# Half of x of batch 0 loaded by hardware queues and cast on chip, x of batch 1 in halves, a new order up to slice 40, and sums of e made on GpSimd

## The chip, the core and the metric

The kernel runs on one core of a Trainium2 chip. A core has TensorE (PE, with its weight load PEld), VectorE (DVE), ScalarE (ACT), GpSimd (POOL) and SyncE (SP), which work through queues of their own, and 16 DMA engines. DMAs issued by SP and ACT go through hardware queues, those issued by GpSimd through a software queue, which can cast float32 to bfloat16 on the way. The metric is the device time of the whole kernel in microseconds, lower is better.

## The reference

Eight batches of cross attention between 512 tokens `x` and 32 state rows per head (8 heads of 64), in both directions, followed by one gated layer over all rows:

```python
scores = scale * x @ state.T;   a  = softmax(scores);   xread = a @ state
scores2 = scale * state @ x.T;  a2 = softmax(scores2);  sread = a2 @ x
rows = concatenate([xread, sread], axis=2)        # (B, H, 512 + 32, 64) -> (4352, 512)
gate = maximum(rows @ w_gate, 0);  val = rows @ w_val   # 512 -> 1536
out = (gate * val) @ w_out                              # 1536 -> 512
```

## The kernel before

Work is in bfloat16 with float32 sums in PSUM. For a batch b, `att_sc` makes the scores for a half kc of the heads, `att_exp` their exponentials `e_sn` (ACT), `att_sum` and `att_scale` the softmax over the states, `a_sn` (DVE). `a_sn` is turned to `ANS`, by PE (`att_T`, `att_out`) in the first three batches and by a DMA transpose later. The value product is folded into the weights: U = state @ w_gate and state @ w_val per head (`c_unit` and `u_unit` on PE, `c_out` and `u_out` to SBUF), so that `gv(b, jf)` gives slice jf (of 12, 128 columns each) of both hidden halves in two PSUM banks. `relu` (ACT) and `mult` (DVE) turn them into `h_sb`. The output product is done in 14 half products a batch (`o_half`, a Winograd scheme of seven products), for which GpSimd makes sums of hidden blocks (`h_sums`, `h_last`, tiles `s`) and of weight blocks (`w_sum`, tiles `t1`, `t2w`, `t4`). PSUM has a ring of six banks for all but the two output accumulators.

The other direction is `sr_mm(b)`: PE multiplies x with `e_sn`, and with `sel`, a matrix of ones for one half of the partitions, it adds `e_sn` over all 512 tokens: for each parity, half kc and group c of 128 tokens one matmul, 16 a batch. `sr_norm` divides one by the other into `br`. These rows go through the hidden layer at the end (`gvs`, `s_step`).

The order is written by hand. A prologue issues the DMAs: the state of the first two batches on SP; on GpSimd's queue x of batch 0 in two halves with a cast, pieces of 256 columns of w_gate and w_val in turn, x of batches 1 and 2 with a cast, the other states, w_out and x of batch 3. A ring of eight semaphores makes a GpSimd DMA wait for the eighth before it. A string `program` then gives the order up to slice 40 (batch 3, slice 4): words such as `xT.0.3` (transpose x of batch 0, head pair 3), `xo.0.3.dve` (its copy, on DVE), `sc.0.0`, `c.0.4`, `co` (copy of U), `ga` and `gb` (the two halves of gv), `re`, `mu`, `oh.0.2`, `hs`, `hl`, `ws`, `nx` (att_scale), `srm` and `srn` (sr_mm, sr_norm), and `spin.n`, n matmuls on an empty tile `warm`. After that a loop over slices runs each output half product 18 slices behind its gv, and `at(b, jf, ...)` hangs the attention of the next batch and the rest on given slices.

Of the kernel before, what the change touches and what calls it, by code (L numbers as in the profile page):

```python
# [16 lines left out]
def kernel(  # L17
# [182 lines left out]
    def att_scale(b, kc):  # L200
        e_v = e_sn[b][:, kc].rearrange("p c (h n) -> p (c h) n", n=Ns)
        nc.vector.tensor_tensor(out=a_sn[b][:, kc].rearrange("p c (h n) -> p (c h) n", n=Ns), in0=e_v,  # L202
                                in1=held["rc", b, kc].to_broadcast([128, NC * HK, Ns]), op=ALU.mult)
# [20 lines left out]
    def sr_mm(b):  # L224

        ps = held["sr", b] = bank("sr_ps")
        e = e_sn[b].rearrange("p k c (j s n) -> p k c j s n", j=2, s=2)
        for kc in range(NK):
            for c in range(NC):
                for j2 in range(2):  # L230
                    j = 2 * kc + j2
                    if b in cast_on_load:
                        for h2 in range(2):
                            q = slot(j, h2)
                            nc.tensor.matmul(ps[64 * h2:64 * h2 + 64, 64 * j + 32 * q:64 * j + 32 * q + 32],
                                             xb[b][:, c, 2 * j + h2], e[:, kc, c, j2, q],
                                             start=(kc == 0 and c == 0 and j2 == 0), stop=False, skip_group_check=True)
# [4 lines left out]
        for parity in range(2):
            for kc in range(NK):
                for c in range(NC):
                    nc.tensor.matmul(ps[:, 256 + 64 * kc:320 + 64 * kc], sel[:, parity],  # L245
                                     e[:, kc, c, :, slot(2 * kc, parity)],
                                     start=False, stop=(parity == 1 and kc == 1 and c == NC - 1), skip_group_check=True)
# [238 lines left out]
    nc.vector.memset(warm, 0.0)
# [42 lines left out]
    program = """
    spin.7 stc.0.2.dve stT.0.2 sto.0.2.1.dve xT.0.0 xT.0.1 xo.0.1.dve xT.0.3 xo.0.3.dve sto.0.2.0.dve  # L530
    xo.0.0.act sc.0.0 ex.0.0 xT.0.2 spin.1 xo.0.2.dve sc.0.1 spin.1 ex.0.1 nr.0.0 c.0.0 nx.0.0 aT.0.0 nr.0.1
    nx.0.1 co.0.0.1.act c.1.0 ao.0.0.act aT.0.1 co.0.0.0.act ga.0.0 co.1.0.1.dve c.0.1 co.1.0.0.act c.1.1
    ao.0.1.dve gb.0.0 co.0.1.0.act ga.0.2 co.1.1.0.act co.0.1.1.dve gb.0.2 re.0.0 mu.0.0 ga.0.3 gb.0.3
    co.1.1.1.dve ga.0.1 gb.0.1 re.0.2 mu.0.2 xT.1.0 re.0.3 mu.0.3 xT.1.2 re.0.1 mu.0.1 xT.1.1 xo.1.1.dve
    xT.1.3 xo.1.3.dve c.0.2 co.0.2.1.dve xo.1.0.act sc.1.0 c.1.2 co.1.2.0.dve xo.1.2.act co.0.2.0.act sc.1.1
    ga.0.4 ga.0.5 gb.0.5 ex.1.0 co.1.2.1.act ex.1.1 c.0.3 gb.0.4 nr.1.0 nx.1.0 aT.1.0 re.0.5 co.0.3.0.act
    mu.0.5 ao.1.0.dve re.0.4 nr.1.1 c.1.3 co.1.3.1.act c.0.4 ga.0.6 co.0.4.0.dve nx.1.1 co.0.3.1.act gb.0.6
    co.1.3.0.act mu.0.4 ga.0.7 co.0.4.1.act re.0.6 gb.0.7 re.0.7 aT.1.1 ao.1.1.dve mu.0.7 ga.0.9 mu.0.6 gb.0.9
    ga.0.8 gb.0.8 re.0.9 ga.1.0 gb.1.0 ga.1.1 gb.1.1 ga.1.6 mu.0.9 re.0.8 re.1.0 mu.1.0 re.1.1 mu.1.1 gb.1.6
    re.1.6 ga.1.3 gb.1.3 mu.0.8 re.1.3 ga.1.2 stT.2.4 mu.1.6 gb.1.2 re.1.2 ga.1.5 gb.1.5 sto.2.4.0.act mu.1.3  # L540
    re.1.5 ga.1.4 mu.1.5 gb.1.4 ga.1.7 gb.1.7 oh.0.0 sto.2.4.1.act re.1.7 re.1.4 xT.2.0 xT.2.2 mu.1.2 c.0.5
    co.0.5.0.act xT.2.3 mu.1.7 xT.2.1 mu.1.4 xo.2.2.dve co.0.5.1.dve xo.2.1.dve c.1.5 hs.0.0 hs.0.1 ga.0.11
    co.1.5.0.dve co.1.5.1.dve xo.2.0.act gb.0.11 re.0.11 mu.0.11 xo.2.3.act ga.0.10 gb.0.10 oh.0.1 sc.2.0
    ga.1.10 gb.1.10 re.0.10 mu.0.10 ws.0.pool ex.2.0 ga.1.11 gb.1.11 re.1.10 re.1.11 u.2.1.0 uo.2.1.0.1.act
    nr.2.0 mu.1.10 uo.2.1.0.0.act nx.2.0 mu.1.11 c.1.4 sc.2.1 ex.2.1 oh.0.2 oc.0.1 u.2.0.0 aT.2.0 ws.1.pool
    co.1.4.0.dve hs.0.2 nr.2.1 ga.1.8 xc.3.0.pool xc.3.1.pool co.1.4.1.act nx.2.1 oh.0.4 uo.2.0.0.0.act gb.1.8
    ws.2.pool re.1.8 oh.0.3 oh.0.5 mu.1.8 xd.4 ga.1.9 oa.0.3 ao.2.0.dve ws.3.pool gb.1.9 hl.0 hs.1.0
    xc.4.0.pool xc.4.1.pool aT.2.1 oh.0.6 ao.2.1.act ga.2.0 uo.2.0.0.1.dve xt.3 re.1.9 mu.1.9 gb.2.0 ga.2.1
    hs.1.2 xt.4 re.2.0 mu.2.0 gb.2.1 re.2.1 ga.2.3 gb.2.3 hs.1.1 ga.2.2 re.2.3 mu.2.3 oc.0.5 gb.2.2 re.2.2
    oh.0.7 oh.0.8 u.2.1.1024 mu.2.1 uo.2.1.1024.0.dve u.2.0.1024 uo.2.0.1024.0.dve oh.0.9 u.2.1.512  # L550
    uo.2.1.512.0.dve uo.2.0.1024.1.act u.2.0.512 oc.0.9 oa.0.9 oh.0.10 oh.0.11 uo.2.0.512.0.act ga.2.5 oh.0.12
    oc.0.11 mu.2.2 ga.2.4 uo.2.0.512.1.dve oh.1.0 uo.2.1.512.1.act gb.2.4 gb.2.5 oh.0.13 xd.5 re.2.4 mu.2.4
    re.2.5 sc.3.0 oh.1.1 srm.0 os.0.11 ga.2.7 ex.3.0 ga.2.6 oa.0.13 mu.2.5 uo.2.1.1024.1.act gb.2.6 nr.3.0
    srn.0 re.2.6 mu.2.6 sc.3.1 ex.3.1 gb.2.7 re.2.7 mu.2.7 nr.3.1 nx.3.0 nx.3.1 aD.3 oc.1.1 ga.2.8 gb.2.8
    u.3.0.0 hs.2.0 oh.1.2 re.2.8 mu.2.8 u.3.0.512 uo.3.0.0.0.act uo.3.0.512.0.act uo.3.0.0.1.dve u.3.1.0
    oh.1.3 hl.1 oa.1.3 oh.1.4 uo.3.1.0.1.dve uo.3.1.0.0.act ga.2.9 uo.3.0.512.1.dve gb.2.9 srm.1 re.2.9 oh.1.5
    mu.2.9 oc.1.5 ga.2.10 srn.1 gb.2.10 re.2.10 mu.2.10 xc.5.0.pool ga.2.11 stT.4.8 sto.4.8.1.act
    sto.4.8.0.dve gb.2.11 re.2.11 mu.2.11 oh.1.6 oh.1.7 u.3.1.1024 uo.3.1.1024.0.act u.3.1.512
    uo.3.1.512.1.dve u.3.0.1024 uo.3.1.512.0.act oh.1.8 uo.3.0.1024.1.dve ga.3.0 gb.3.0 uo.3.0.1024.0.act
    hs.2.1 hs.2.2 ga.3.1 xc.5.1.pool re.3.0 gb.3.1 re.3.1 ga.3.3 oh.1.9 mu.3.0 mu.3.1 oc.1.9 oa.1.9  # L560
    uo.3.1.1024.1.dve ga.3.2 gb.3.2 re.3.2 srm.2 gb.3.3 re.3.3 oh.1.10 mu.3.2 oh.1.11 sc.4.0 ex.4.0 srn.2
    nr.4.0 nx.4.0 oc.1.11 os.1.11 xt.5 mu.3.3 xd.6
    """
# [91 lines left out]
```

## Time and profile before

| | |
|---|---|
| median of the runs | 227.91 us (227.42 to 228.1, 3 runs) |
| profiled execution | 226.67 us, span 224.9 us |
| PE busy | 212.3 us |
| GpSimd busy | 149.9 us |
| first gv matmul | 13.76 us |
| first product with w_out | 35.93 us |
| last PE matmul of the chain ends | 220.60 us |

The span is what the trace covers; the profiled execution's own time is 1.8 us longer. Starts are microseconds from the span's start. A row in order of time gives start, duration, engine, line, operation and tiles, and in brackets the idle time before it and what ended it. Line numbers are those of the kernel before; in the changed kernel the same lines stand further down.

### The profile page before, as it was taken

The numbers are of one execution on the slowest core, as the hardware profiler recorded it, in microseconds if no ns is written. First come the engines' busy times: TensorE is split into PE (matmuls) and PEld (weight loads), VectorE is DVE, ScalarE is ACT, GpSimd is POOL, SyncE is SP. The second block draws the span as 40 slices with busy tenths as digits, with TensorE's granted clock in tenths as the row PEclk, the third lists the DMA queues.
The fourth block names the chain that finished last, engine by engine and source line by source line (L and its number), as shares of the span: only waits on it lengthen the run. The fifth ranks groups of instructions, "written<-read, shape, count | busy, mean of one in ns | idle before, by whom it ended". The sixth has DMA issues, their size and how long they took to land.

```text
span 224.9 us, 5527 instructions
## 1 busy us (share of the span) xinstructions
PE 212.3 (94%) x2219; PEld 140.1 (62%) x2251; DVE 160.0 (71%) x278; ACT 120.1 (53%) x226; POOL 149.9 (67%) x141
## 2 busy tenths in 40 slices
...
GB/s 94 171 192 196 197 195 271 62 50 278 3 111 266 138 3 85 201 230 4 62 227 228 3 72 184 74 3 91 63 82 1 81 62 47 4 95 50 47 26 208
DMA packets 42329, 25.06 MB, mean 111 GB/s; under 512 B 18784, under 2 KB 41824, under 8 KB 42304
## 3 DMA queue, kind: packets, MB, share of 16 engines
...
## 4 chain that ended last, share of the span: by engine, by line
PE 78%; DMA 8%; DVE 5%; issue 3%; ACT 2%; POOL 2%; another core or an unknown queue 0%; ACTq 0%; DVEq 0%; POOLq 0%
PE gv_ps L299 30%; PE w_ps L394 18%; PE z_ps L394 13%; DMA wv_sb<-in_moe_w_val_dram 5%; PE gv_ps L317 5%; PE up L274 4%; DMA wg_sb<-in_moe_w_gate_dram 3%; PE sr_ps L245 2%; ACT g_sb L326 2%; PE zs_ps L394 1%; DVE h_sb L330 1%; DVE a_sn L202 1%; PE ws_ps L394 1%; PE sc_ps L186 1%; PE sr_ps L240 1%
## 5 line engine op out<-in xcount | busy, mean ns | idle before, releaser
L330 DVE TENSOR_TENSOR h_sb<-gv_ps,g_sb 128x512 bf16<-128x512 f32 (+1 forms) x108 | 69.0, 656 | 35.1 <-ACT g_sb L326 26.1
L299 PE MATMUL gv_ps<-ans,U 128*128 128x512 bf16 x353 | 92.1, 379 | 1.9 <-DVE U L294 0.2
L326 ACT ACTIVATE g_sb<-gv_ps 128x512 bf16<-128x512 f32 (+1 forms) x108 | 61.9, 576 | 44.2 <-PE gv_ps L299 21.1
L394 PEld LDWEIGHTS <-h_sb 128*128 128x128 bf16 x510 | 49.4, 98 | 15.9 <-issue 1.5
L360 POOL TENSOR_TENSOR s<-h_sb 128x512 bf16<-128x512 bf16 x24 | 28.1, 1172 | 43.9 <-DVE h_sb L330 43.8
L299 PEld LDWEIGHTS <-U 128*128 128x128 bf16 x384 | 35.7, 98 | 31.1 <-issue 0.8
L369 POOL TENSOR_TENSOR h_sb<-h_sb,s 128x512 bf16<-128x512 bf16 x24 | 27.0, 1154 | 7.3 <-PE z_ps L394 7.3
L404 ACT COPY o_sb<-w_ps 128x512 f32<-128x512 f32 x32 | 18.8, 586 | 21.9 <-PE w_ps L394 19.2
L361 POOL TENSOR_TENSOR s<-s,h_sb 128x512 bf16<-128x512 bf16 x24 | 28.0, 1167 | 1.9
L362 POOL TENSOR_TENSOR h_sb<-h_sb 128x512 bf16<-128x512 bf16 x24 | 28.1, 1172 | 0.0
L394 PE MATMUL w_ps<-wo_sb,h_sb 128*128 128x256 bf16 x192 | 26.2, 273 | 0.0
L284 ACT CAST U<-up 128x512 bf16<-128x512 f32 x37 | 19.9, 595 | 11.8 <-PE up L274 11.8
L394 PE MATMUL z_ps<-wo_sb,h_sb 128*128 128x256 bf16 x186 | 24.4, 273 | 0.0
L394 PEld LDWEIGHTS <-s 128*128 128x128 bf16 x204 | 19.2, 98 | 7.7 <-issue 2.8
L284 DVE CAST U<-up 128x512 bf16<-128x512 f32 x35 | 22.3, 682 | 1.6 <-PE up L274 1.5
L410 DVE TENSOR_TENSOR o_sb<-z_ps,o_sb 128x512 f32<-128x512 f32 (+1 forms) x23 | 15.5, 673 | 4.5 <-PE z_ps L394 2.7
L196 DVE TENSOR_REDUCE cs<-e_sn 128x16 f32<-128x512 bf16 x16 | 10.8, 678 | 5.6 <-ACT e_sn L190 5.6
L202 DVE TENSOR_TENSOR a_sn<-e_sn,rc 128x512 bf16<-128x512 bf16 x16 | 14.2, 893 | 0.4
L190 ACT ACTIVATE e_sn<-sc_ps 128x512 bf16<-128x512 f32 x16 | 9.6, 600 | 8.5 <-PE sc_ps L186 8.4
L394 PE MATMUL w_ps<-t2w,s 128*128 128x256 bf16 x96 | 13.1, 273 | 0.1
L394 PE MATMUL z_ps<-t,s 128*128 128x256 bf16 x90 | 12.0, 273 | 0.1
L394 PE MATMUL w_ps<-t,h_sb 128*128 128x256 bf16 x96 | 12.0, 273 | 0.0
...
## 6 DMA issues: line engine op xcount, KB each, us to landing
...
xf<-in_x_dram SPq DMA_DIRECT2D x4, 1024.0 KB, 6.8
...
xb<-in_x_dram POOLq DMA_DIRECT2D x2, 512.0 KB, 10.6
xf<-in_x_dram POOLq DMA_DIRECT2D x1, 1024.0 KB, 19.5
...
```

What stands on the lines that cost most here:

```text
L202: nc.vector.tensor_tensor(out=a_sn[b][:, kc].rearrange("p c (h n) -> p (c h) n", n=Ns), in0=e_v, in1=held["rc", b, kc].to_broadcast([128, ...
L284: copy[eng](out=U[b][:, w, kc, lo:lo + 512], in_=held["u", b, w, lo][kc])
L299: nc.tensor.matmul(ps[w], U[b][:, w, kc, f0:f0 + 128], ANS[b][:, kc].rearrange("p c t -> p (c t)"), start=(kc == 0), stop=(kc == NK - 1))
L326: nc.scalar.activation(out=g_sb[:, 0:n], in_=ps[0][:, 0:n], func=AF.Relu)
L330: nc.vector.tensor_tensor(out=dst, in0=ps[1][:, 0:n], in1=held["g", b, jf][:, 0:n], op=ALU.mult)
L360: tt(out=s_block(b, 1, i), in0=a21, in1=a22, op=ALU.add)
L361: tt(out=s_block(b, 2, i), in0=s_block(b, 1, i), in1=a11, op=ALU.subtract)
L362: tt(out=a21, in0=a11, in1=a21, op=ALU.subtract)
L369: {"dve": nc.vector, "pool": nc.gpsimd}[eng].tensor_tensor(out=a12, in0=a12, in1=s_block(b, 2, i), op=ALU.subtract)
L394: nc.tensor.matmul(ps[:, HM * c:HM * c + HM], a[:, i, 128 * c:128 * c + 128], w[:, i], start=(i == 0 and (p in ("p1", "p2", "p5") and c == ...
L404: nc.scalar.copy(out=o_sb, in_=held["acc", b, "w", 0])
L410: nc.vector.tensor_tensor(out=o_sb[:, cols], in0=banks[c if isinstance(c, int) else 0][:, cols], in1=o_sb[:, cols], op=ALU.add)
```

## The change

x of batch 0: heads 0 and 1 come as float32 on ACT's hardware queue, heads 2 and 3 on SP's behind the state, heads 4 to 7 on GpSimd's queue with a cast as before. Two new steps `xh.0.dve` and `xh.1.act` cast the first four heads. x of batch 1 comes in two DMAs. x of batch 3 is issued by a step `xg.3`. `sr_pre` adds the four token groups of `e_sn` on GpSimd in float32 (three passes over 128x256) and has ACT round the sum to bfloat16; `sr_low` has GpSimd write what the rounding left. `sr_mm` then uses these two parts, 8 matmuls with `sel` instead of 16, for the batches that have them: 3 to 7. `att_scale` can run on GpSimd, and does for (2, 1), (3, 1) and (4, 0); the casts (3, 0) and (5, 0) of x go from GpSimd to ACT. The program is in a new order, with three more warm-up matmuls.

```diff
+    def sr_pre(b):
+        t = small.tile([128, NK, 128], FP32, name="es_f", tag="es_f", bufs=1)
+        for c in range(1, NC):
+            nc.gpsimd.tensor_tensor(out=t, in0=t if c > 1 else e_sn[b][:, :, 0], in1=e_sn[b][:, :, c], op=ALU.add)
+        es = held["es", b] = small.tile([128, 2, NK, 128], BF16, name="es", tag="es", bufs=1)
+        nc.scalar.copy(out=es[:, 0], in_=t)
+        held["es_f", b] = t
+
+    def sr_low(b, eng="pool"):
+        es = held["es", b]
+        {"dve": nc.vector, "pool": nc.gpsimd}[eng].tensor_tensor(out=es[:, 1], in0=held["es_f", b], in1=es[:, 0],
+                                                                op=ALU.subtract)
...
+        if ("es", b) in held:
+            for parity in range(2):
+                for kc in range(NK):
+                    for part in range(2):
+                        es = held["es", b][:, part, kc].rearrange("p (j s n) -> p j s n", j=2, s=2)
+                        nc.tensor.matmul(ps[:, 256 + 64 * kc:320 + 64 * kc], sel[:, parity],
+                                         es[:, :, slot(2 * kc, parity)],
...
+    x0_dma(nc.scalar, xf[0], 0, 2)
     state_dma(nc.sync, st_f, 0, 2)
-    x_dma_cast(0, 2)
+    x0_dma(nc.sync, xf[0], 2, 4)
+    x0_dma(nc.gpsimd, xb0, 4, H)
...
         if i == 1:
-            x_dma_cast(1)
+            x_dma_cast(1, 2)
...
-    x_dma(3, (nc.gpsimd,))
...
-    spin.7 stc.0.2.dve stT.0.2 sto.0.2.1.dve xT.0.0 xT.0.1 xo.0.1.dve xT.0.3 xo.0.3.dve sto.0.2.0.dve
+    stc.0.2.dve spin.7 stT.0.2 sto.0.2.1.act spin.1 xh.0.dve spin.1 xT.0.0 sto.0.2.0.dve xh.1.act xT.0.1
...
     for b in range(3, B):
+        at(*((b, 5) if b < B - 1 else (b, 2)), sr_pre, b)
+        at(*((b, 5) if b < B - 1 else (b, 2)), sr_low, b, "pool")
         at(*((b + 1, 0) if b < B - 1 else (b, 4)), sr, b)
```

GpSimd's queue at the start (`xb` is x in bfloat16, `id` and `sel` are constants, `wg_sb` and `wv_sb` the weights), before:

```order
L116 DMA xb<-in_x_dram 128x4x256 x2
masks.py:197 MEMSET id_94 128x128
...
L120 DMA wv_sb<-in_moe_w_val_dram 128x4x256
L116 DMA xb<-in_x_dram 128x8x256
L120 DMA wg_sb<-in_moe_w_gate_dram 128x4x256
```

and with the change:

```order
L520 DMA xb<-in_x_dram 128x4x256
masks.py:197 MEMSET id_94 128x128
...
L120 DMA wv_sb<-in_moe_w_val_dram 128x4x256
L116 DMA xb<-in_x_dram 128x4x256 x2
L120 DMA wg_sb<-in_moe_w_gate_dram 128x4x256
```

One x DMA fewer stands ahead of the constants and weights, and one more between the second and the third pair of weights.

DVE's queue at the start (`stT` is the turned state, `xT` the turned x), before:

```order
L487 MEMSET stT 128x1024
L129 CAST st_b<-st_f 128x256
L143 COPY stT<-stT_ps 64x2x2x32 x2
L175 COPY xT<-xT_ps 128x4x128 x2
L143 COPY stT<-stT_ps 64x2x2x32 x2
L175 COPY xT<-xT_ps 128x4x128
```

and with the change:

```order
L512 MEMSET stT 128x1024
L129 CAST st_b<-st_f 128x256
L523 CAST xb<-xf 128x512
L143 COPY stT<-stT_ps 64x2x2x32 x2
L175 COPY xT<-xT_ps 128x4x128 x3
L196 TENSOR_REDUCE cs<-e_sn 128x16
```

A cast of x comes in, and the state's second pair of copies has gone to ACT, so that none stands behind copies of x.

GpSimd in the middle of the program, from the third `h_sums` of batch 0 to the first of batch 1, before:

```order
L362 TENSOR_TENSOR h_sb<-h_sb 128x2x256
L151 CAST xb<-xf 128x4x4x64 x2
L338 TENSOR_TENSOR t_100<-wo_sb,t2w 128x1536
L338 TENSOR_TENSOR wo_sb<-wo_sb 128x6x256
L369 TENSOR_TENSOR h_sb<-h_sb,s_775 128x2x256 x3
L360 TENSOR_TENSOR s_970<-h_sb 128x512
```

and with the change, where the casts of batch 4 also move ahead of batch 1's sums:

```order
L387 TENSOR_TENSOR h_sb<-h_sb 128x2x256
L151 CAST xb<-xf 128x4x4x64
L202 TENSOR_TENSOR a_sn<-e_sn,rc 128x512
L363 TENSOR_TENSOR t_100<-wo_sb,t2w 128x1536
L363 TENSOR_TENSOR wo_sb<-wo_sb 128x6x256
L394 TENSOR_TENSOR h_sb<-h_sb,s_686 128x2x256 x3
L151 CAST xb<-xf 128x4x4x64 x2
L385 TENSOR_TENSOR s_997<-h_sb 128x512
```

One cast of x has become a multiplication `a_sn`; the other cast of batch 3 is on ACT.

More of the change, by code (lines that the diff above doesn't have):

```diff
@@ L198, in att_sum, with att_scale @@
         nc.vector.reciprocal(out=rc, in_=cs)
-    def att_scale(b, kc):
+    def att_scale(b, kc, eng="dve"):
         e_v = e_sn[b][:, kc].rearrange("p c (h n) -> p (c h) n", n=Ns)
-        nc.vector.tensor_tensor(out=a_sn[b][:, kc].rearrange("p c (h n) -> p (c h) n", n=Ns), in0=e_v,
+        (nc.gpsimd if eng == "pool" else nc.vector).tensor_tensor(out=a_sn[b][:, kc].rearrange("p c (h n) -> p (c h) n", n=Ns), in0=e_v,
                                 in1=held["rc", b, kc].to_broadcast([128, NC * HK, Ns]), op=ALU.mult)
@@ L241, in sr_mm @@
                                      start=(kc == 0 and c == 0 and j2 == 0), stop=False, skip_group_check=True)
+        if ("es", b) in held:
[5 more added lines that the diff above has]
+                                         es[:, :, slot(2 * kc, parity)],
+                                         start=False, stop=(parity == 1 and kc == 1 and part == 1),
+                                         skip_group_check=True)
+            return
         for parity in range(2):
@@ L487, with x0_dma, x0_cast @@
     nc.vector.memset(stT, 0.0)
+    cast_on_load.add(0)
+    xb_alloc(0)
+    xf[0] = xin.tile([128, H, NC, D], FP32, name="xf", tag="xf")
+    xb0 = xb[0].rearrange("p (h c d) -> p h c d", h=H, c=NC)
+    xb[0] = xb[0].rearrange("p (h c d) -> p c h d", h=H, c=NC)
+    def x0_dma(eng, dst, lo, hi):
+        eng.dma_start(out=dst[:, lo:hi], in_=x[0, lo:hi].rearrange("h (p c) d -> p h c d", c=NC))
+    def x0_cast(i, eng):
+        copy[eng](out=xb0[:, 2 * i:2 * i + 2], in_=xf[0][:, 2 * i:2 * i + 2])
+    x0_dma(nc.scalar, xf[0], 0, 2)
     state_dma(nc.sync, st_f, 0, 2)
-    x_dma_cast(0, 2)
+    x0_dma(nc.sync, xf[0], 2, 4)
+    x0_dma(nc.gpsimd, xb0, 4, H)
     nc.scalar.activation(out=tiny, in_=nc.const_aps.tensor(0.0, (128, 1), FP32), func=AF.Exp)
@@ L526 @@
              "gb": lambda b, jf: gv(b, jf, (1,)), "re": relu, "mu": mult, "oh": o_half, "oc": o_c, "oa": o_a, "os": o_s,
-             "hs": h_sums, "hl": h_last, "ws": w_sum, "xd": lambda b: x_dma(b, (nc.sync,)), "xc": x_cast,
-             "xt": x_trans_dma, "aD": att_aT_dma, "srm": sr_mm, "srn": sr_norm}
+             "hs": h_sums, "hl": h_last, "ws": w_sum, "xd": lambda b: x_dma(b, (nc.sync,)), "xg": lambda b: x_dma(b, (nc.gpsimd,)),
+             "xh": x0_cast, "xc": x_cast,
+             "xt": x_trans_dma, "aD": att_aT_dma, "srp": sr_pre, "srl": sr_low, "srm": sr_mm, "srn": sr_norm}
@@ L535 @@
[L535 to L559, printed above, removed]
```

41 lines of the change are left out of this document (33 added, 8 removed).

## The prediction

> **What bounds the kernel now.** I read the page's busy times, then the stages, then the chain of waits, then the first 15 us and the GpSimd lane in order of time. The sum below is made against the profiled execution: 226.67 us, of which 224.9 are span. The runs' median is 227.91, 1.24 above it, so I take differences from the profile and apply them to the median. A difference under 0.3% (0.7 us) can't be told from none.
>
> ```profile
> PE 212.3 (94%) x2219; PEld 140.1 (62%) x2251; DVE 160.0 (71%) x278; ACT 120.1 (53%) x226; POOL 149.9 (67%) x141
> ```
> ```profile
> 2.00:3.00 1.00, 1.00 (x4) 0.43 (x3) 0.21 (x2) 0.22 (x2) 1.00 (x3) 1.00 0.66 118
> 3.00:4.00 1.00, 1.00 (x4) 0.18 (x2) 0.34 (x1) 0.00 (x0) 0.87 (x5) 1.00 0.97 97
> 4.00:5.00 1.00, 0.93 (x5) 0.40 (x4) 0.04 (x1) 0.00 (x0) 1.00 (x4) 1.00 1.40 186
> ...
> 64.00:75.00 11.00, 9.89 (x168) 6.56 (x170) 10.47 (x17) 5.24 (x11) 10.77 (x10) 1.00 1.06 227
> ...
> 100.00:120.00 20.00, 19.84 (x211) 13.27 (x213) 16.32 (x28) 11.10 (x21) 13.25 (x13) 1.00 0.45 116
> ```
> The columns are the stretch, its length, the busy time of PE, PEld, DVE, ACT and POOL, granted clock, DMA share and GB/s. In the steady loop PE is busy 19.84 of 20 us: work taken off PE there is time. In 64 to 75 PE lacks 1.1 us, and GpSimd is full. The start is another regime, by the chain of waits:
>
> ```profile
> 5.54 6.76 DMA wg_sb<-in_moe_w_gate_dram
> ...
> 12.58 11.98 DMA wv_sb<-in_moe_w_val_dram
> ```
> From 5.54 to 24.56 the chain is weights on their way.
>
> **Term 1, the start.** These rows are in order of time (start, duration, engine, line, operation, and in brackets the wait before it).
>
> ```profile
> 0.74 0.45 SPq L95 DMA_DIRECT2D st_f<-in_state_dram  x1
> 1.19 3.17 PE L516 MATMUL warm_ps<-warm 128*128 128x512 bf16 x7 [1.19 <-DVE warm L486]
> 1.27 1.70 POOL L116 DMA_DIRECT2D xb<-in_x_dram  x2 [0.82 <-POOLq L639]
> 3.00 0.34 DVE L129 CAST st_b<-st_f 128x256 bf16<-128x256 f32 x1 [0.79 <-DMA st_f<-in_state_dram]
> 4.04 0.77 POOL L120 DMA_DIRECT2D wg_sb<-in_moe_w_gate_dram  x1
> 4.29 0.64 PE L136 MATMUL stT_ps<-id,st_b 128*64 128x128 bf16 x4
> 5.58 1.06 PE L169 MATMUL xT_ps<-id,xb 128*64 128x128 bf16 x16 [0.65 <-DMA xb<-in_x_dram]
> 7.35 0.64 PE L169 MATMUL xT_ps<-id,xb 128*64 128x128 bf16 x8 [0.71 <-DMA xb<-in_x_dram]
> 8.63 0.59 PE L186 MATMUL sc_ps<-stT,xT 128*128 128x64 bf16 x8 [0.64 <-DVE stT L143]
> 11.28 0.41 PE L274 MATMUL upc<-wg_sb,stT 64*32 64x256 bf16 x8
> 11.28 0.74 POOL L120 DMA_DIRECT2D wg_sb<-in_moe_w_gate_dram  x1 [0.37 <-DMA wv_sb<-in_moe_w_val_dram]
> 12.58 0.74 POOL L120 DMA_DIRECT2D wv_sb<-in_moe_w_val_dram  x1 [0.56 <-DMA wg_sb<-in_moe_w_gate_dram]
> 13.76 0.59 PE L299 MATMUL gv_ps<-ans,U 128*128 128x512 bf16 x2
> 13.92 0.74 POOL L120 DMA_DIRECT2D wg_sb<-in_moe_w_gate_dram  x1 [0.60 <-DMA wv_sb<-in_moe_w_val_dram]
> ```
> From 11.28 on, a GpSimd DMA waits for the landing of the eighth before it; these landings are 1.30 and 1.34 us apart, so the queue delivers one 256 KB piece (512 KB read) per 1.33 us, in order. Heads 4 to 7 of x now go first on it and heads 0 to 3 leave it: the transposes of heads 6 and 7 waited until 7.35 for the second x DMA, while the first had landed by 5.58. That is up to 1.8 us earlier for this piece and for all weights behind it, which are also issued one DMA (0.85) sooner; splitting x of batch 1 adds one issue of 0.85 behind the fourth weight piece, hidden because the queue waits for landings soon after. But the same 512 KB now travel on SP's and ACT's queues. What is really won is DMA time that lay idle: against a share of 1.40 the stretches 2 to 3 and 3 to 4 lack 0.74 and 0.43, together 1.17 / 1.40 = 0.84 us. I take **-0.85**; ends: 0 (the new transfers push the old ones back in full) and -1.8.
>
> The engines can follow. The state's 128 KB, issued at 0.74, were there at 3.00; 256 KB of x should be there near 3.5 and the second quarter, behind the state on SP, near 4.2 (estimates). The 128x256 cast took 0.34, so a 128x512 one about 0.65: done before 5.0 on DVE and ACT. PE leaves the state's transposes at 4.93, runs two more warm-up matmuls (3.17 / 7 = 0.45 each) and starts on x at 5.8 instead of 5.58: nothing won there. The gain comes next: heads 6 and 7 no longer wait until 7.35, and scores, held at 8.63 by the state's second copy standing behind three others on DVE, start near 7.6. Over the second scores and the spins, the first gv matmul comes at about 13.0 instead of 13.76, which agrees with the landings. The ACT table load slips behind a DMA issue of about 0.45 and is needed only near 8.
>
> The Trainium skill, page "DMA: Bandwidth & Descriptors", section "Issuing engines are not separate DMA queues", speaks against more: DMAs from scalar, sync and gpsimd run on the same 16 engines and interleave, so several issuers save only issuing time. The shares of 0.66 and 0.97 before 4 us agree that there is little room; by the rule the term would lie near its 0 end, which is the second rival.
>
> **Term 2, the new order up to slice 40.** PE's own work there stays, but for three warm-up matmuls that stand in waits. The GpSimd lane, DVE and PE around 70 us:
>
> ```profile
> 28.75 1.15 POOL L360 TENSOR_TENSOR s<-h_sb 128x512 bf16<-128x512 bf16 x1 [4.34 <-DVE h_sb L330]
> 69.23 1.16 POOL L362 TENSOR_TENSOR h_sb<-h_sb 128x512 bf16<-128x512 bf16 x1
> 69.48 3.02 DVE L202 TENSOR_TENSOR a_sn<-e_sn,rc 128x512 bf16<-128x512 bf16 x2
> 70.35 1.60 POOL L360 TENSOR_TENSOR s<-h_sb 128x512 bf16<-128x512 bf16 x1
> 70.46 0.82 PE L394 MATMUL w_ps<-t2w,s 128*128 128x256 bf16 x6
> 73.15 0.68 PE L235 MATMUL sr_ps<-e_sn,xb 128*64 128x32 bf16 x32 [1.01 <-DVE h_sb L330]
> 85.79 1.03 POOL L151 CAST xb<-xf 128x1024 bf16<-128x1024 f32 x1
> 95.10 1.15 POOL L360 TENSOR_TENSOR s<-h_sb 128x512 bf16<-128x512 bf16 x1 [8.27 <-DVE h_sb L330]
> ```
> PE's one long wait (1.01 at 73.15) is for a product that stood behind two multiplications of 1.51 each on DVE. One of the two goes to GpSimd, so this wait should go. What is late next is GpSimd: from 28.75 to 86.8 it runs nearly without a gap, and PE takes the sums s at 70.46, just as the lane ends them (70.39). On this lane three multiplications come and two casts go to ACT: at 1.15 (same size, two inputs) and 1.03, 3.45 - 2.06 = +1.4. It started when PE had made the first products, so it starts earlier by term 1. I take half of the wait, **-0.5**; ends -1.3 (other short waits between 36 and 75 too) and +1.4 (the lane's growth all reaches PE).
>
> **Term 3, sums of e.** For batches 3 to 7, 16 matmuls with sel become 8.
>
> ```profile
> 108.78 2.02 POOL L151 CAST xb<-xf 128x1024 bf16<-128x1024 f32 x2
> 115.27 0.60 ACT L326 ACTIVATE g_sb<-gv_ps 128x512 bf16<-128x512 f32 x1 [0.86 <-PE gv_ps L299]
> 172.66 0.63 PE L245 MATMUL sr_ps<-e_sn,sel 128*128 128x64 bf16 x16
> 173.12 1.03 PE L299 MATMUL gv_ps<-ans,U 128*128 128x512 bf16 x4
> 175.28 1.16 POOL L362 TENSOR_TENSOR h_sb<-h_sb 128x512 bf16<-128x512 bf16 x1
> 176.14 0.60 ACT L326 ACTIVATE g_sb<-gv_ps 128x512 bf16<-128x512 f32 x1 [0.21 <-PE gv_ps L299]
> 179.66 0.63 PE L245 MATMUL sr_ps<-e_sn,sel 128*128 128x64 bf16 x16
> 180.13 1.03 PE L299 MATMUL gv_ps<-ans,U 128*128 128x512 bf16 x3
> L338 POOL TENSOR_TENSOR t<-wo_sb 128x1536 bf16<-128x1536 bf16 x1 | 3.1, 3097 | 0.0
> L467 ACT COPY sr_sb<-ws_ps 128x256 f32<-128x256 f32 x4 | 1.5, 372 | 4.6 <-PE ws_ps L394 4.6
> ```
> Sixteen occupy PE from 172.66 to 173.12, 0.46 us; half is 0.23, five times **-1.15** (other end 0, if waits take its place).
>
> **Term 4, what the sums cost elsewhere.** GpSimd gets four passes over 128x256 per batch. From 1.15 at 512 and 3.10 at 1536 elements, 256 make 1.15 - 256 x 1.9 ns = 0.66 each (ends 0.4 and 1.15, float32 output being new). For batches 4 to 6 the adds follow the casts that end at 110.8 and are done at 112.8; ACT comes to its copy (0.37, from the 128x256 row) behind the relu that ends at 115.87, finds them ready, and GpSimd's last pass ends at 116.9, before the sums that it starts at 117.3. Batch 7 is tight: GpSimd is free at 176.44, the adds end at 178.4, but ACT's copy stands ahead of the relu that ran at 176.14. This relu waits until 178.8; PE needs its bank only at 180.13. The last pass ends near 179.5; PE wants it at 179.66. So **+0.2**; ends 0 and, at 1.15 a pass, 176.44 + 3.45 + 0.37 + 1.15 = 181.4, that is +1.8.
>
> Sum: -0.85 - 0.5 - 1.15 + 0.2 = -2.3: 224.4 for a profiled execution, 225.6 for the median.
>
> **Rivals.** *Start and order give more*: the weights really come 1.8 earlier and the short waits go too (-1.8 - 1.3 - 1.15 + 0.2 = -4.05): 223.9. For it: 7.35 against 5.58. Against: the same bytes in the same window.
>
> *The transfers only interleave*: the weights land as before, term 1 is 0, or the casts on chip only replace the wait. -1.45 remains: 226.5. For it: a share of 1.40 from 4 us on.
>
> *Slower: the GpSimd lane becomes the bound between 28 and 87 us.* Its place is the sums s that PE takes at 70.46 the moment they exist. If a broadcast multiplication takes T there, the lane grows by 3T - 2.06. With terms 1 to 4 at -2.3 it decides at T = 1.45; at T = 2.3, twice the nearest row, it is +4.84, in all +2.5: 230.4. For it: GpSimd rows of 1.60 beside DVE's a_sn. Against: the second batch's multiplication is paid for by a cast of 1.03, and 8.27 us idle at 95.10 take up the rest. The Trainium skill's "GPSIMD Engine Reference", section "Key points", names this contention, with DVE instructions that have two SBUF inputs; the 1.51 of a_sn agrees.
>
> **How the numbers follow.** The sum 0.55 (225.6, own range 224.8 to 226.4), more 0.17, interleaving 0.16, the lane 0.12. Interleaving at 226.5 is faster by 0.6% but may lose another microsecond to the ends of terms 2 and 4, so half of it counts as the same; of the lane, which begins at no change, a sixth. Faster 0.80, same 0.10, slower 0.10. The range runs from just under the second case to no change, 223.7 to 227.9.
>
> **What would show it.** Term 1: the wait for x at 7.35 gone, first gv matmul near 13.0, the wait for wv_sb at 24.56 near 23.7. Term 2: no 1 us wait of PE for DVE near 73; GpSimd's first long gap beginning no later than 88. Term 3: 40 fewer sel matmuls and PE's steady stretches still over 98% busy. Term 4: GpSimd's four passes 0.6 to 0.7 each, no PE wait near 178. The prediction is wrong if weights land as before and GpSimd's multiplications take over 1.5.

## The result and the profile after

The changed kernel takes 223.92 us in the median of four runs (222.89 to 224.39), the kernel before 228.0 beside it. The ratio of the runs, which isn't the quotient of the two medians (0.982), is 0.985, 95% interval 0.980 to 0.989. Two later comparisons gave 0.985 (0.982 to 0.987) and 0.985 (0.981 to 0.988). So the change is worth 3.4 to 3.5 us by the ratios, 3.1 to 4.1 us by the medians, where the forecast had 2.3. The time is that of the first rival, "start and order give more"; the gain by the ratios lies between the sum's 2.3 and that rival's 4.05.

The profiled execution took 224.17 us, span 222.1 (before 226.67 and 224.9). The page's busy times, then the same stretches as before with four more, in the same columns:

```profile
PE 213.4 (96%) x2214; PEld 139.3 (63%) x2214; DVE 150.3 (68%) x263; ACT 128.7 (58%) x247; POOL 164.1 (74%) x162
```
```profile
2.00:3.00 1.00, 1.00 (x4) 0.43 (x3) 0.21 (x1) 0.73 (x2) 0.92 (x4) 1.00 0.49 134
3.00:4.00 1.00, 1.00 (x4) 0.18 (x2) 0.00 (x0) 0.00 (x0) 0.94 (x4) 1.00 1.13 369
4.00:5.00 1.00, 0.38 (x2) 0.02 (x1) 0.55 (x2) 0.00 (x0) 1.00 (x3) 1.00 1.31 260
64.00:75.00 11.00, 11.00 (x177) 7.20 (x176) 8.42 (x16) 7.85 (x16) 10.84 (x10) 1.00 0.70 205
100.00:120.00 20.00, 20.00 (x194) 13.30 (x187) 16.30 (x28) 12.23 (x24) 16.87 (x18) 1.00 0.58 136
25.00:40.00 15.00, 14.93 (x132) 7.48 (x131) 11.20 (x19) 11.05 (x23) 11.83 (x8) 1.00 1.26 219
40.00:60.00 20.00, 19.91 (x207) 12.70 (x206) 12.37 (x20) 15.65 (x30) 18.96 (x14) 1.00 0.38 95
60.00:80.00 20.00, 20.00 (x268) 12.79 (x267) 13.73 (x24) 14.70 (x29) 19.68 (x18) 1.00 0.57 146
80.00:95.00 15.00, 15.00 (x168) 9.79 (x166) 11.79 (x21) 8.23 (x17) 10.82 (x12) 1.00 0.74 172
```

The last four stretches in the profile before:

```profile
25.00:40.00 15.00, 14.76 (x129) 7.55 (x131) 11.97 (x21) 10.11 (x22) 10.68 (x8) 1.00 1.36 229
40.00:60.00 20.00, 19.25 (x193) 11.59 (x193) 16.46 (x26) 12.72 (x24) 19.84 (x13) 1.00 0.36 101
60.00:80.00 20.00, 18.78 (x257) 12.22 (x259) 16.83 (x29) 10.74 (x22) 19.77 (x18) 1.00 0.66 146
80.00:95.00 15.00, 14.84 (x151) 9.96 (x152) 12.25 (x23) 8.62 (x16) 6.67 (x7) 1.00 0.39 94
```

Between 25 and 95 us PE lacks 0.24 + 0.75 + 1.22 + 0.16 = 2.37 us in these rows, and 0.16 now. Not all of the 2.37 was idle time: the profile before holds 2219 matmuls and 2251 weight loads, and where the record of a gv matmul is missing, a hole of about 0.05 us is left. e9 below has the old order with all records (2251 of both):

```profile
25.00:40.00 15.00, 14.81 (x132) 7.50 (x131) 11.58 (x21) 10.11 (x22) 10.93 (x8) 1.00 1.31 226
40.00:60.00 20.00, 19.57 (x196) 11.79 (x195) 16.44 (x26) 12.95 (x25) 19.81 (x13) 1.00 0.35 95
60.00:80.00 20.00, 19.00 (x261) 12.22 (x260) 16.86 (x29) 10.75 (x22) 19.69 (x19) 1.00 0.65 146
80.00:95.00 15.00, 15.00 (x153) 9.96 (x152) 12.26 (x22) 8.45 (x16) 6.66 (x7) 1.00 0.39 89
```

It lacks 0.19 + 0.43 + 1.00 = 1.62 us. So the idle time of PE went from some 1.6 us to 0.16. (In 100 to 120 too, e9 has PE busy for 20.00, where the profile before showed 19.84.) DVE's load in 40 to 80 fell from 33.3 to 26.1 us, ACT's rose from 23.5 to 30.4, and GpSimd's, which was feared, fell from 39.6 to 38.6.

To place the difference, each profile is cut at four PE instructions: A, the first gv matmul of slice 6 of batch 0; B and C, the sr products of batches 3 and 6; D, the first matmul that takes the rows `br`. A stretch between two of them leaves out when PE began. All profiles of this study, us:

| profile | start to A | A to B | B to C | C to D | D to end | span |
|---|---|---|---|---|---|---|
| before | 24.84 | 79.29 | 68.06 | 20.54 | 32.17 | 224.9 |
| changed | 24.78 | 77.43 | 67.36 | 20.39 | 32.14 | 222.1 |
| e1 old load | 25.65 | 77.41 | 67.36 | 20.42 | 31.96 | 222.8 |
| e2 no sums | 25.55 | 77.19 | 68.06 | 20.54 | 31.96 | 223.3 |
| e3 sums alone | 24.59 | 79.16 | 67.36 | 20.41 | 32.08 | 223.6 |
| e4 state first | 24.43 | 77.41 | 67.36 | 20.41 | 31.89 | 221.5 |
| e5 changed | 23.90 | 78.03 | 67.36 | 20.41 | 32.00 | 221.7 |
| e6 no sums | 23.78 | 77.24 | 68.05 | 20.54 | 31.79 | 221.4 |
| e7 on DVE | 24.88 | 77.68 | 67.36 | 20.42 | 31.96 | 222.3 |
| e8 one moved | 25.95 | 78.29 | 68.06 | 20.53 | 31.97 | 224.8 |
| e9 load alone | 24.68 | 79.28 | 68.06 | 20.53 | 31.95 | 224.5 |
| e10 order alone | 24.84 | 77.88 | 68.06 | 20.53 | 31.99 | 223.3 |
| e11 copy later | 24.85 | 77.23 | 67.36 | 20.07 | 32.09 | 221.6 |
| e12 changed | 23.82 | 78.51 | 67.36 | 20.39 | 32.22 | 222.3 |

Wherever the code in them is the same, B to C repeats to 0.01 and C to D to 0.03. Start to A does not: the changed kernel alone has 24.78, 23.90 and 23.82. Nor does A to B in the new order: 77.43, 78.03 and 78.51, for which e5 and e12 below give a likely reason. So the sums from batch 4 on can be read from one profile, but the start only from medians of several runs.

The start after the change, PE and DVE in order of time:

```profile
1.19 3.17 PE L554 MATMUL warm_ps<-warm 128*128 128x512 bf16 x7 [1.19 <-DVE warm L511]
4.45 0.48 DVE L129 CAST st_b<-st_f 128x256 bf16<-128x256 f32 x1 [2.24 <-DMA st_f<-in_state_dram]
4.98 0.63 PE L136 MATMUL stT_ps<-id,st_b 128*64 128x128 bf16 x4 [0.62 <-DVE st_b L129]
6.51 1.49 PE L169 MATMUL xT_ps<-id,xb 128*64 128x128 bf16 x24
7.93 0.72 PE L186 MATMUL sc_ps<-stT,xT 128*128 128x64 bf16 x8
13.08 0.40 PE L218 MATMUL aT_ps<-id,a_sn 128*128 128x128 bf16 x4 [1.10 <-DVE a_sn L202]
13.41 0.59 PE L324 MATMUL gv_ps<-ans,U 128*128 128x512 bf16 x2
```

PE's wait for x at 7.35 is gone. The state, issued at 0.74 as before, is in use at 4.45 instead of 3.00: it now shares the DMA engines with two quarters of x, which 369 GB/s between 3 and 4 us show (97 before). By the Trainium skill, page "DMA: Bandwidth & Descriptors", section "Issuing engines are not separate DMA queues", transfers of several issuers interleave on the same 16 engines; the state's delay of 1.45 us agrees with it.

### The profile page after: what moved, and what is told of

It reads as the page before. It is cut to its first block, busy times and chain, and to the rows that moved or that the text cites. A ratio compares the mean times of both kernels' runs of the same rounds, so it can differ in the third digit from the quotient of the medians.

```text
span 222.1 us, 5525 instructions
## 1 busy us (share of the span) xinstructions
PE 213.4 (96%) x2214; PEld 139.3 (63%) x2214; DVE 150.3 (68%) x263; ACT 128.7 (58%) x247; POOL 164.1 (74%) x162
## 4 chain that ended last, share of the span: by engine, by line
PE 82%; POOL 7%; ACT 4%; DVE 3%; DMA 2%; issue 1%; DVEq 0%; POOLq 0%
PE gv_ps L324 34%; PE w_ps L419 17%; PE z_ps L419 12%; PE gv_ps L342 5%; PE up L299 4%; PE sc_ps L186 2%; DMA st_f<-in_state_dram 2%; POOL s L386 2%; POOL s L385 2%; POOL h_sb L387 2%; POOL h_sb L394 2%; PE zs_ps L419 1%; ACT g_sb L351 1%; PE ws_ps L419 1%; PE xT_ps L169 1%; PE upc L299 1%
## 5 line engine op out<-in xcount | busy, mean ns | idle before, releaser
L324 PE MATMUL gv_ps<-ans,U 128*128 128x512 bf16 x384 | 94.9, 379 | 0.2
L309 ACT CAST U<-up 128x512 bf16<-128x512 f32 x43 | 22.7, 595 | 10.0 <-PE up L299 10.0
L309 DVE CAST U<-up 128x512 bf16<-128x512 f32 x29 | 18.4, 684 | 1.6 <-PE up L299 1.6
L299 PEld LDWEIGHTS <-stT 64*32 64x32 bf16 x480 | 6.1, 89 | 7.1 <-issue 4.6
```

Of the source, the lines that this page charges most:

```text
L299: nc.tensor.matmul(dst[kc][q:q + 32], stT[r:r + 64, b, j, 32 * sl:32 * sl + 32], wsb[r:r + 64, j, lo:lo + n], start=True, stop=True)
L309: copy[eng](out=U[b][:, w, kc, lo:lo + 512], in_=held["u", b, w, lo][kc])
L324: nc.tensor.matmul(ps[w], U[b][:, w, kc, f0:f0 + 128], ANS[b][:, kc].rearrange("p c t -> p (c t)"), start=(kc == 0), stop=(kc == NK - 1))
```

## The experiments

Every ratio is to the kernel before on the same chip, with its 95% interval, and gains in us are worked out from the ratios unless medians are named. The changed kernel ran beside e6 to e8 (as e5) and beside e9 to e11 (as e12), but not beside e1 to e4, whose ratios are held against its 0.985.

**e1: the old loading of x of batch 0.**

```diff
-    x0_dma(nc.scalar, xf[0], 0, 2)
     state_dma(nc.sync, st_f, 0, 2)
-    x0_dma(nc.sync, xf[0], 2, 4)
-    x0_dma(nc.gpsimd, xb0, 4, H)
+    x_dma_cast(0, 2)
...
-    ... spin.1 xh.0.dve spin.1 xT.0.0 sto.0.2.0.dve xh.1.act xT.0.1
+    ... spin.1 spin.1 xT.0.0 sto.0.2.0.dve xT.0.1
```

> The changed kernel, but x of batch 0 comes as before: two casting DMAs on GpSimd's queue, no casts on chip. Theory (the start gives little, because the state now lands at 4.45 instead of 3.00 and the chain of engines, not the weights, sets the pace up to 25 us): about 0.3 us slower than the changed kernel, in a profile a span near 222.4. Rival (the new order only works because the weights land 1.5 us earlier): the wait of PE for wv_sb near 24.6 comes back and 1.2 us or more are lost, span near 223.3.

Measured: 224.49 us, ratio 0.989 (0.987 to 0.991). Against 0.985 for the changed kernel, the new loading is worth about 0.9 us, with intervals that overlap. That lies between the theory (0.3) and the rival (1.2 or more), and so does the span of 222.8. PE's wait for the weights is back:

```profile
25.41 0.30 PE L299 MATMUL upc<-wv_sb,stT 64*32 64x256 bf16 x8 [0.61 <-DMA wv_sb<-in_moe_w_val_dram]
```

The stretch A to B, 77.41, is the changed kernel's: the loading acts on the start alone.

**e2 and e6: no sums on GpSimd**, the same kernel on two chips.

```diff
-        at(*((b, 5) if b < B - 1 else (b, 2)), sr_pre, b)
-        at(*((b, 5) if b < B - 1 else (b, 2)), sr_low, b, "pool")
```

> The changed kernel without the sums of e on GpSimd: all batches use 16 matmuls with sel. Theory (the steady loop is bound by PE, so 5 x 0.23 us come back, less the 0.2 wait in batch 7): 0.9 to 1.15 us slower than the changed kernel, all of it after 92 us. Rival (the matmuls were hidden behind other waits, and the gain past 92 us is the order's): 0 to 0.3 us.

> The changed kernel without the sums of e on GpSimd once more, beside the changed kernel on the same chip. Its profile gave 90.08 us from the first sums s of batch 3 to those of batch 7 against 89.23 with them, so theory: 0.8 to 1.1 us slower than the changed kernel in the medians. Rival (what the matmuls save is given back in the program, where the copy on ACT and four passes for batch 3 come in): 0.2 to 0.5 us slower.

Measured: ratios 0.987 (0.985 to 0.989) and 0.987 (0.984 to 0.989): by these the sums are worth some 0.4 to 0.5 us, at the limit of what they can tell; both theories (0.9 to 1.15, 0.8 to 1.1) missed, and e6's rival holds. By the stretches: B to C 68.06 without and 67.36 with them, 0.233 for each of the three products in it, those of batches 3 to 5. C to D, with the products of batches 6 and 7, gains only 0.15. A to B, in which GpSimd and ACT make the sums for batch 3, is 0.2 longer with them than without.

**e3: the sums alone.** The kernel before with `sr_pre`, `sr_low` and the shorter `sr_mm`, hung on the same slices.

> The kernel before with the sums of e on GpSimd and nothing else. Theory: 0.9 to 1.15 us faster than before. Rival (in the old order the new passes on GpSimd and the copy on ACT come at a bad moment for the next batch's a_sn on DVE): under 0.5 us faster.

Measured: 226.47 us, ratio 0.997 (0.995 to 0.998), that is -0.73 us (-0.4 to -1.1), which leaves both the theory and the rival open. B to C is again 67.36 and C to D 20.41. A to B is not longer here (79.16 against 79.29), and in this order ACT waits for GpSimd ahead of its rounding copy once alone, in batch 7 (2.9 us), and not in batch 3.

**e4: the state ahead of x.**

```diff
-    x0_dma(nc.scalar, xf[0], 0, 2)
     state_dma(nc.sync, st_f, 0, 2)
-    x0_dma(nc.sync, xf[0], 2, 4)
+    x0_dma(nc.sync, xf[0], 0, 2)
     x0_dma(nc.gpsimd, xb0, 4, H)
     nc.scalar.activation(out=tiny, in_=nc.const_aps.tensor(0.0, (128, 1), FP32), func=AF.Exp)
+    x0_dma(nc.scalar, xf[0], 2, 4)
```

> The changed kernel, but ACT's x DMA is issued after its table load instead of ahead of it, and carries heads 2 and 3, while SP's carries heads 0 and 1 behind the state. Theory (the state's landing at 4.45 is the head of the chain): the state lands near 3.1, the first gv matmul comes about 0.6 us earlier than 13.41 and up to 0.6 us are won in all. Rival (the wait is passed on: scores, a_sn and the casts of U set the pace): the state lands earlier but the end moves by less than 0.2 us.

Measured: 224.08 us, ratio 0.987 (0.985 to 0.989). The state comes at 4.01 in its profile, so the edit took back only 0.44 of the 1.45 us, and not the way to 3.1 that was expected. The first gv matmul is at 12.29, but e5, without the edit, has it at 12.37. The runs show no gain over the changed kernel: the rival holds for these 0.44 us, and what the whole delay costs stays open.

**e5 and e12: the changed kernel again**, on two chips.

> The changed kernel itself, beside the next runs on one chip, for its spread. Theory (what varies between runs is when the weights land in the first 25 us): ratio to before near 0.985; in the profile the distance from the first matmuls of slice 6 of batch 0 (24.78 in the first profile) to the first sums s of batch 3 (93.42) is 68.6 again, whatever the start is. Rival (the order's gain varies too): the distance moves by more than 0.3.

> The changed kernel again, for comparison with the three others on one chip: ratio 0.985; stretches 77.4 to 78.0 and 20.4. If the parts add up, its gain is that of the loading alone, the order alone and the sums alone (0.7 us) together.

Measured: 223.63 and 224.04 us, both 0.985. In these profiles PE reaches A 0.9 earlier than in the first, and A to B is 0.6 and 1.1 longer, so e5's rival (the order's gain varies too) holds, and e12's 78.51 lies outside the 77.4 to 78.0 expected. GpSimd shows where, first in the changed kernel's first profile:

```profile
38.01 3.10 POOL L363 TENSOR_TENSOR t2w<-wo_sb,t 128x1536 bf16<-128x1536 bf16 x1
```

then in e5:

```profile
38.81 3.10 POOL L363 TENSOR_TENSOR t2w<-wo_sb,t 128x1536 bf16<-128x1536 bf16 x1 [1.65 <-DMA wo_sb<-in_moe_w_out_dram]
```
```profile
43.62 0.40 PE L218 MATMUL aT_ps<-id,a_sn 128*128 128x128 bf16 x4 [0.49 <-DVE a_sn L202]
```

and in e12:

```profile
38.95 3.09 POOL L363 TENSOR_TENSOR t2w<-wo_sb,t 128x1536 bf16<-128x1536 bf16 x1 [1.79 <-DMA wo_sb<-in_moe_w_out_dram]
```
```profile
54.10 0.82 PE L419 MATMUL w_ps<-wo_sb,h_sb 128*128 128x256 bf16 x6 [0.44 <-POOL wo_sb L363]
68.28 0.41 PE L299 MATMUL up<-wg_sb,stT 64*32 64x512 bf16 x8 [0.32 <-DVE h_sb L355]
```

The landing of w_out's second half is late next: where GpSimd waits for it, it goes on between 38.0 and 39.6, and this doesn't follow PE: e6 and e12 reach A at 23.78 and 23.82, and go on at 37.98 and 38.95. Over the nine profiles with the new order (e7, with its own edit there, aside): where the sum `t2w` starts 13.2 to 14.2 us after A, A to B is 77.2 to 77.4; where it starts 14.7 to 15.1 after (e10, e5, e12), A to B is 0.6 to 1.1 longer. The PE waits shown make up 0.5 of the 0.6 in e5 and 0.8 of the 1.1 in e12. This is a relation over profiles; no edit moved w_out alone.

**e7: the three multiplications back on DVE**, in the new order.

```diff
-    nx.2.1.pool ... nx.3.1.pool ... nx.4.0.pool
+    nx.2.1 ... nx.3.1 ... nx.4.0
```

> The changed kernel with the multiplications (2,1), (3,1) and (4,0) on DVE instead of GpSimd. Theory (the 1 us wait of PE near 73 went because one multiplication left DVE): a wait of PE for DVE of 0.5 to 1 us comes back in the middle of the program and the kernel is 0.5 to 1.0 us slower. Rival (the new order keeps PE supplied in any case): under 0.3 us, no PE wait over 0.3 between 25 and 92.

Measured: 224.03 us, ratio 0.986 (0.984 to 0.989); A to B 77.68, 0.25 more than in the changed kernel's first profile, and no PE wait over 0.3 us there. The theory missed: most of the order's gain doesn't come from the multiplications. (The medians beside each other differ by 0.4 us, 224.03 and 223.63, which the intervals don't separate.)

**e8: one multiplication moved in the old order.**

```diff
-    ... nr.3.1 nx.3.0 nx.3.1 aD.3 ...
+    ... nr.3.1 nx.3.0 nx.3.1.pool aD.3 ...
```

> The kernel before with one multiplication, (3,1), moved from DVE to GpSimd, and nothing else. Theory: PE's wait of 1.01 us for DVE at 73.15 goes and about 0.9 us is won. Rival (GpSimd's lane, which has no gap there, hands the wait on): PE waits elsewhere and under 0.4 us is won.

Measured: 225.68 us, ratio 0.995 (0.992 to 0.997); A to B 78.29, 1.0 less than before. PE's row at the place where it waited 1.01 at 73.15:

```profile
73.45 0.68 PE L235 MATMUL sr_ps<-e_sn,xb 128*64 128x32 bf16 x32
```

No bracket: the wait is gone, and its whole length is won. (The row stands later because PE reached A later, at 25.95.) The multiplication itself was not cheap on GpSimd:

```profile
71.47 1.50 POOL L202 TENSOR_TENSOR a_sn<-e_sn,rc 128x512 bf16<-128x512 bf16 x1
```

It ran beside the other one, which took 1.49 on DVE from 70.57 on.

**e9: the new loading alone**, in the old order.

```diff
-    x_dma_cast(0, 2)
+    x0_dma(nc.scalar, xf[0], 0, 2) ... as in the changed kernel
...
-    spin.7 stc.0.2.dve stT.0.2 sto.0.2.1.dve xT.0.0 xT.0.1
+    spin.7 stc.0.2.dve stT.0.2 xh.0.dve sto.0.2.1.dve xh.1.act xT.0.0 xT.0.1
```

> The kernel before with only the new loading: x of batch 0 by three queues, two casts on DVE and ACT, x of batch 1 in halves; old order, no sums on GpSimd. Against the changed kernel with the old loading, the new loading was worth some 0.9 us in the medians. If that is a term of its own, this kernel takes 0.9 us less than the one before (ratio about 0.996), and the stretch from the first gv matmul of slice 6 of batch 0 to the sr product of batch 3 stays 79.2 us. Rival: the old order, with the state's second copy behind the copies of x and PE's wait of 1.01 at sr_ps, can't use the earlier weights: ratio 0.998 to 1.000, and the stretch grows by what the start wins.

Measured: 225.58 us, ratio 0.994 (0.991 to 0.997), -1.3 us (-0.7 to -2.0). The old order takes the gain too: A to B 79.28, as before. The rival fell. The twelve runs lie in two groups, eight at 225.2 to 226.3 and four at 227.0 to 227.3; why stays open.

**e10: the new order alone**, with the old loading of x of batch 0 and without the sums; x of batch 1 in two DMAs and the step `xg.3` stay.

> The changed kernel with the old loading of x of batch 0 and without the sums on GpSimd: of the large parts only the new order is left (with the multiplications on GpSimd and the casts on ACT). If the profiles' stretches tell the truth, the order alone gives -2.1 us: ratio 0.991, stretch 77.2 us. By the prediction's term it gives -0.5: ratio 0.998. If the order only pays with an earlier start, it lies between.

Measured: 225.39 us, ratio 0.991 (0.988 to 0.994): -2.0 us. A to B is 77.88 in its profile, with the late w_out (39.59) just described; -1.4 there, while e2 and e6 show -2.1 with the same order. The prediction's -0.5 (ratio 0.998) lies outside the interval.

**e11: the rounding copy later.**

```diff
-        at(*((b, 5) if b < B - 1 else (b, 2)), sr_low, b, "pool")
-        at(*((b + 1, 0) if b < B - 1 else (b, 4)), sr, b)
+        at(*((b, 6) if b < B - 1 else (b, 4)), sr_low, b, "pool")   # now with ACT's copy
+        at(*((b + 1, 0) if b < B - 1 else (b, 6)), sr, b)
```

> The changed kernel with ACT's rounding copy and GpSimd's last pass issued a slice later than the three adds for batches 3 to 6 and two slices later for batch 7, whose sr product moves from slice 4 to slice 6. Theory: where the sums cost time, it is because this copy stands ahead of a relu on ACT and waits there for GpSimd's adds (2.0 us in batch 3, 2.9 us in batch 7). Then batch 3 loses its 0.2 (stretch 77.2 instead of 77.4) and the stretch from the sr product of batch 6 to the first gvs matmul falls from 20.4 to 20.1: together 0.5 us less than the changed kernel. Rival: the adds themselves, by sharing the memory port with DVE, cost this time: then nothing changes, within 0.1 us in the stretches.

Measured: 223.62 us, ratio 0.984 (0.979 to 0.989), against 224.04 for the changed kernel beside it. The medians don't separate the two; the stretches do: A to B 77.23 and C to D 20.07, as the theory had it (77.2 and 20.1), so the rival fell. Batch 7 in the changed kernel, on GpSimd, ACT and PE:

```profile
176.45 0.67 POOL L271 TENSOR_TENSOR es<-es_f,es 128x256 bf16<-128x256 f32 x1 [0.52 <-ACT es L265]
```
```profile
175.97 0.41 ACT L265 CAST es<-es_f 128x256 bf16<-128x256 f32 x1 [2.89 <-POOL es_f L263]
176.28 0.59 ACT L351 ACTIVATE g_sb<-gv_ps 128x512 bf16<-128x512 f32 x1
```
```profile
176.81 0.19 PE L247 MATMUL sr_ps<-es,sel 128*128 128x64 bf16 x1
177.17 0.36 PE L247 MATMUL sr_ps<-es,sel 128*128 128x64 bf16 x7 [0.17 <-POOL es L271]
```

and in e11:

```profile
175.38 0.60 ACT L350 ACTIVATE g_sb<-gv_ps 128x512 bf16<-128x512 f32 x1
175.87 0.41 ACT L269 CAST es<-es_f 128x256 bf16<-128x256 f32 x1
```
```profile
179.25 0.63 PE L240 MATMUL sr_ps<-e_sn,xb 128*128 128x64 bf16 x16
179.72 0.40 PE L247 MATMUL sr_ps<-es,sel 128*128 128x64 bf16 x8
```

In the changed kernel ACT stands 2.89 us on the copy, with a relu behind it, and PE waits for the last pass. In e11 a relu goes first, the copy waits for nothing, and PE finds the sums ready. e11 moved the copy and batch 7's product together, so the parts of the 0.3 us in C to D weren't told apart; the 0.2 in A to B is the copy's, since only it and the last pass moved there (ACT still waits 1.52 us on it in batch 3, but one relu more is done by then). For this the profiles with an early `t2w` are compared: 77.41 to 77.43 with the copy as in the changed kernel (the first profile, e1, e4), 77.19 to 77.24 without it or with it later (e2, e6, e11).

## Why the prediction was right or wrong

**The direction was right, the size 1.2 us short by the ratios (0.8 to 1.8 by the medians), and one term has most of that.** The parts alone add up within their intervals: loading -1.3 (e9), order -2.0 (e10), sums -0.7 (e3) make -4.0, all together -3.4 to -3.5.

**Term 1, the start (-0.85): right in size, for a reason that failed.** e1 gives 0.9, e9 1.3 with 0.7 as the smaller end. The number was taken from DMA time that lay idle between 2 and 4 us, and this time wasn't filled: the DMA shares there add up to 1.63 before (0.66 and 0.97) and to 1.62 after (0.49 and 1.13). So the size was luck in part. What did happen is that the weights came earlier. The second DMA of w_out waits until the fourth piece of w_val has landed. It went out before at

```profile
22.20 0.82 POOL L124 DMA_DIRECT2D wo_sb<-in_moe_w_out_dram  x1 [0.55 <-DMA wv_sb<-in_moe_w_val_dram]
```

and goes out with the change at

```profile
20.64 0.82 POOL L124 DMA_DIRECT2D wo_sb<-in_moe_w_out_dram  x1 [0.52 <-DMA wg_sb<-in_moe_w_gate_dram]
```

(The second bracket names w_gate, but both wait for the semaphore of that piece of w_val, whose last update is at 21.92 and 20.36.) The fifth piece of w_val, for which PE waited, lands by its semaphore at 24.56 before, and in the changed kernel's three profiles at 23.06, 23.62 and 23.54, where 23.7 was expected. In all five profiles with the old loading it lands at 24.3 to 25.4, in seven of the nine with the new one at 23.1 to 24.2; in e2 and e11 it came as late as with the old one (25.3 and 24.5). The queue that casts has one DMA of 256 KB less ahead of the weights, and the first weight DMA is issued at 3.27 instead of 4.04; what each of the two gives wasn't told apart.

The signs were half right. PE's wait for x went, and scores moved from 8.63 to 7.93, with 7.6 expected. PE's wait for wv_sb, then 24.56, is in none of the changed kernel's three profiles, and comes back with the old loading in e1 (0.61 us; with the new one e2 and e4 show 0.17 and 0.18). The first gv matmul is at 13.41, 12.37 and 12.26 in these profiles, where 13.0 was expected: a spread between executions wider than the term. The forecast's landing of the state at 3.00 was wrong by 1.45 us, and that of x (near 3.5 and 4.2) by about 1 us each: both quarters land 3.9 us after their issue at 0.73 and 1.25, and the casts that were to be done before 5.0 end at 5.25 on DVE and 6.71 on ACT. The rule on issuing engines was seen at work in the state's delay, yet the term didn't fall to its 0 end: the second rival, no gain from the transfers, is refuted by e9.

**Term 2, the new order (-0.5): the term that was mis-sized.** It is -2.0 (-1.3 to -2.8) by e10's runs and -2.0 to -2.1 by the stretches of e2 and e6. The step that failed is "I take half of the wait": the whole wait of 1.01 went (e8 shows that this alone is worth 1.0), and PE's other idle time between 25 and 95 us, some 0.5, went with it (1.62 by e9, 0.16 now). Even the end of -1.3 was too small. The last 0.6 shows nowhere as idle time. A gv matmul is shown 0.38 us long, while four in a row take 1.03, so the next can start 0.22 after it, and a stall of up to 0.16 leaves no gap. From each start to the next, the same 172 gv matmuls between A and B take 37.95 us in e9 and 37.49 in e6.

The other half of the step failed as well: the GpSimd lane was said to grow by 1.4 with PE near it. PE was not as near as the prediction read: the row that ends at 70.39 writes h_sb, and the last row that wrote s ended at 69.28, so that PE took these sums at 70.46 1.2 us after they were there. And the multiplications take less than the 1.15 assumed:

```profile
L202 POOL TENSOR_TENSOR a_sn<-e_sn,rc 128x512 bf16<-128x512 bf16 x3 | 3.1, 1044 | 2.1 <-ACT g_sb L351 2.1
L202 DVE TENSOR_TENSOR a_sn<-e_sn,rc 128x512 bf16<-128x512 bf16 x13 | 9.3, 712 | 0.4
```

1.04 each, so that 3 x 1.04 replaces 2 x 1.03 of casts; and the lane's next long gap still begins at 85.8 (88 was the limit set). What the term should have started from stood in the windows: all idle time of PE in the stretch that is ordered anew, not half of the one wait above 1 us. What of the order brings the second microsecond wasn't isolated; by e7 it isn't the multiplications (0.25). The copies that went from DVE to ACT are the largest shift of load, but no run moves them alone.

**Term 3, the sums (-1.15): right.** 0.233 us per batch against 0.23, and 40 sel matmuls fewer. In B to C it came in full; elsewhere part of it was lost again, which is term 4.

**Term 4 (+0.2): the mechanism right, two places instead of one.** For batch 7 the copy stood ahead of a relu as foretold (it starts at 175.97, not 178.4; the whole program runs 2.6 earlier by then). The forecast took the relu's delay as free because PE needed its bank late; together with the wait for the last pass it cost 0.3. And in the new order the same thing happens in batch 3 (ACT waits 2.0 us there), which the forecast, looking at batches 4 to 6, left out: 0.2. In the old order (e3) the copy doesn't wait there, and A to B isn't longer. So the term is +0.5; terms 3 and 4 together are -0.65 instead of -0.95. The passes themselves were sized well:

```profile
L263 POOL TENSOR_TENSOR es_f<-es_f,e_sn 128x256 f32<-128x256 f32 x10 | 7.7, 767 | 0.8
L271 POOL TENSOR_TENSOR es<-es_f,es 128x256 bf16<-128x256 f32 x5 | 3.3, 670 | 6.2 <-ACT es L265 6.2
L263 POOL TENSOR_TENSOR es_f<-e_sn 128x256 f32<-128x256 bf16 x5 | 3.3, 666 | 0.0
L247 PE MATMUL sr_ps<-es,sel 128*128 128x64 bf16 x40 | 2.1, 193 | 0.2 <-POOL es L271 0.2
L255 PE MATMUL sr_ps<-e_sn,sel 128*128 128x64 bf16 x48 | 1.9, 194 | 0.0
```

0.67 for ten of the twenty passes and 0.77 for the ten that read and write float32, against an estimate of 0.66; 40 + 48 sel matmuls instead of 128, the 40 fewer that were named.

**The rivals.** The first, "start and order give more", gave the right time, 223.9, by half of the right reason: the order gave more, beyond even that rival's -1.3, and the start did not give its 1.8. That the time agrees to 0.1 is luck. The slower one, the lane as the bound, fell: it needed a multiplication of 1.45, and 1.04 was measured. But e8 has one of 1.50 beside DVE: the figure depends on whether two of them run side by side, and in the changed kernel they don't. The contention that the Trainium skill's "GPSIMD Engine Reference", section "Key points", names is there, on both sides: `a_sn` on DVE averages 0.71 now against 0.89 before, when two of them took 1.51 each beside GpSimd, and the sum s on GpSimd took 1.60 beside them against 1.15.
